# Attention loop: each head's sum, reciprocal, shares and transposes one step later, bias sums in odd steps

## The chip, the cores and the metric

The kernel runs on one core of one Trainium2 chip. The metric is the device time of one execution in microseconds (us). Engines are named as in the profile: PE (TensorE matmul), PEld (its weight loads), DVE (VectorE), ACT (ScalarE), POOL (GpSimd) and SP (SyncE, which issues the DMAs).

## The reference

Three stages stand one behind the other: attention with a position bias that a small network makes, a gated product with two weight matrices, and a block with softmax and layer norm. The attention has 2 batches, 8 heads, 576 positions and 64 dimensions per head; then there are 1152 rows of 512, with inner sizes 1536 and 1024.

```python
rel = pos[:, None] - pos[None, :]
x = (log1p(abs(rel)) / log1p(maximum(pos[:, None], 1)))[..., None]
bias = relu(x @ w1 + b1) @ w2                      # 1 -> 32 hidden -> 8 heads
scores = q @ k.T / sqrt(D) + bias.transpose(2, 0, 1)
attn = exp(scores - max); attn = attn / (attn.sum(-1) + 1e-9)
x = (attn @ v) as 1152 rows of 512
x = ((x @ w_a) * (x @ w_b)) @ w_out
h = x @ w_in;  solu = h * softmax(h)
out = (layer_norm(solu) * g_ln) @ w_out2
```

## The kernel before

**Tiles and heads.** The 576 query positions of a batch are four row tiles of 128 and a rest of 64. There are nine units: four row tiles times two batches, and one unit that holds the rests of both batches. A unit has eight heads, so the list `steps` holds 72 heads.

**The loop.** `for n in range(len(steps) + 5)` (L635) works on several heads at once. For each step n the string of letters in `ORDER` (L27) whose key is the largest that is at most n says which parts are issued and in which order. All engines take their instructions in the order in which they are issued, so the string sets the order on every engine. The letters:

- `s` scores of head n (L400, PE: tile `s`, two halves, with the high part `qhi` of q and its correction `qlo`);
- `b` biased, head n-1 (L419, DVE: adds `bias` to `s`, writes `e` and the row's extreme `nm`);
- `p` powers, head n-1 (L426, ACT: exponential in place, row sums);
- `a` summed_powers, head n-1 (L430, POOL: adds the small constant, tile `rec`);
- `h` shares, head n-2 (L435, DVE: reciprocal of `rec`; L436, POOL: multiplies `e`). In step 3, `g` and `f` make the sum and shares of an older head in an order of their own;
- `t` turned, head n-3 (PE transposes `pt` at L444 and, for the second head of a pair, `ptt` at L453; the copy `et` is ACT's for an even head, L447, DVE's for an odd one, L449; `ett` is ACT's, L455);
- `v` values, in odd steps: a pair of heads whose first is n-4 (L473, PE: tile `px`);
- `i` and `j`: high part (ACT, `xhi`, L479) and correction (DVE, `xlo`, L484) of a finished unit's output, in steps 4 mod 8;
- `k` and `l`: high part (`kst`, `qhi`) and correction (`qlo`, DVE, L327) of k and q for later units;
- `u` bias_sums and `o` bias_out: sums of a group of bias rows (L366, PE: tile `bps` from four tiles `h`), its store and its DMA;
- `x` everything else at that step's number: loads, copies of q and k (`nat_q` L280 on POOL, `nat_k` and `arena_hi` L277 and L278), their transposes `tp_q` and `tp_k` (L290), the bias network's hidden tiles `h` (L356 on DVE, L358 on ACT; two in step n-2 and two in n-1 for sums in step n), clearing of q tiles by POOL, and in the last unit the conversion of the first weights.

**What else sets the order.** A bias group's step is 16i + 2r, for the first row of groups a number from `SECOND_T`, for the last row one from `LAST_T` (L30, L31). The scores and the bias sums take turns in one PSUM pool of two buffers (`ps_s`); the later gated blocks `pm` use that pool too. Transposes have a pool of three buffers, `e` one of three, `et` one of two.

**End of the loop.** The weights come as 64-bit numbers, read as pairs of 32-bit words (`words`, L94) and rebuilt in single precision by ACT, POOL and DVE (L98, L102, L111, L113, L114); the first four pieces are rebuilt inside the loop by `first_one`, at the steps that `FIRST` lists (L609 and L611 make the high part and the correction, tile `first`). Three gated blocks `pm` (L132, 24 matmuls each, named by weight piece and row group) stand in the loop too, by `EARLY` in steps 72 (0,0), 74 (0,1) and 75 (1,0); their products are ACT's copy `one` (L151), DVE's `g` (L152), ACT's `gh` (L154) and DVE's `gl` (L156). Behind the loop the other weights are loaded into a pool that takes the attention's space, and blocks (1,1), (0,2), (1,2), (2,0) and so on follow.

Of the kernel before, what the change touches and what calls it, by code (L numbers as in the profile page):

```python
# [22 lines left out]

ORDER = {0: "kbvioljpatsxu", 2: "kbvioljptsxu", 3: "kbglfviojptshaxu", 4: "khbvioljpatsxu", 55: "khbilospajtvxu"}  # L27

KEYS = (4, 5, 6, 7, 7, 8, 9, 10, 11, 11)
SECOND_T = (5, 7, 9, 10, 12, 13, 14)  # L30
LAST_T = (48, 50, 52, 54)  # L31

HIDDEN = (("vvva", "vvva", "vvva", "vvva", "vvva", "vvva", "vvva", "vvva"),
          ("vvvv", "avvv", "avav", "avvv", "avav", "avvv", "avav", "avvv"), ("vvvv", "avvv"))
# [20 lines left out]
def tile_kernel(ctx, tc, q, k, v, w1, b1, w2, w_a, w_b, w_out, w_in2, w_out2, g_ln, psi, rpsi, out):  # L55
# [9 lines left out]
    NC = S // P  # L65
# [98 lines left out]
    with ExitStack() as actx:  # L164
# [56 lines left out]
        for g in range(4):  # L221
            r = slice(g * HID, (g + 1) * HID)
# [124 lines left out]
        def bias_hidden(T, quads=range(4)):  # L347

            it, r, c = place(T)
            for qd in quads:  # L350
                t0 = it * P + r + 16 * qd
                h = hp.tile([P, S], F32, tag="h", name=f"h_{T}_{qd}")
                win = tb[:, OFF - t0 - c:OFF - t0 - c + S]
                sc = nb[:, c, t0 // 16:t0 // 16 + 1]
                if HIDDEN[min(it, 2)][T % len(HIDDEN[min(it, 2)])][qd] == "v":
                    nc.vector.tensor_scalar(h, win, sc, 0.0, op0=ALU.add, op1=ALU.max)  # L356
                else:
                    nc.scalar.activation(h, win, AF.Relu, bias=sc)  # L358
                bias_w.setdefault(T, []).append(h)

        def bias_sums(T):

            bps = ps_s.tile([P, 2, 512], F32, tag="s", name=f"bps_{T}")
            for qd, h in enumerate(bias_w[T]):
                for a in range(2):
                    nc.tensor.matmul(bps[32 * qd:32 * qd + 32, a, 0:SH], w2bd, h[:, a * SH:(a + 1) * SH], start=True, stop=True)  # L366
            bias_w[T] = bps

        def bias_out(T, send=True):

            it, r, c = place(T)
            if it not in bias_t:
                bias_t[it] = big.tile([P, H, S], F32, tag="big", name=f"bias_{it}")
            st = stp.tile([P, S], F32, tag="st", name=f"st_{T}")
            k = 9 * c + 2 * it + r // 64
            nc.scalar.activation(st.rearrange("p (a j) -> p a j", a=2), bias_w.pop(T)[:, :, 0:SH], AF.Copy, scale=rp[:, k:k + 1])
            bias_w[T] = st
            if send:
                bias_sent(T)
# [78 lines left out]
        def values(u, p):  # L458

            it, bs = units[u]  # L460
            px = st_[u][0]
            et = [st_.pop(("et", u, 2 * p + j)) for j in range(2)]
            ett = st_.pop(("ett", u, p))
            n = P // len(bs)
            for c in range(NC + 1):
                for j, half in ((j, half) for j in range(2) for half in range(2)):

                    rows = slice(j * D + half * HID, j * D + (half + 1) * HID)
                    for m, b in enumerate(bs):
                        cols = slice(m * n, (m + 1) * n)  # L470
                        lhsT = (vsb[:, b, c] if c < NC else vtl[:, b])[:, p, j, half * HID:(half + 1) * HID]
                        rhs = et[j][:, c, cols] if c < NC else ett[:, cols]
                        nc.tensor.matmul(px[rows, p, cols], lhsT, rhs, start=(c == 0 and m == 0), stop=(c == NC), skip_group_check=True)  # L473
# [17 lines left out]
        def later(n, f, *args):  # L491
            extra.setdefault(n, []).append((f, args))
# [11 lines left out]
        for b in range(B):  # L504
            for g in range(2):
                i = b * 2 + g
# [72 lines left out]
            later(8 * (len(units) - 1) + j, clear_q, len(units) - 1, i // 4, i // 2 % 2, i % 2)  # L579
        for T in range(N0 + 1, S // 16):  # L580
            i, r = divmod(T - N0, N0)
            n = LAST_T[r] if i == NC - 1 else 16 * i + (SECOND_T[r - 1] if i == 0 else 2 * r)
            for g in range(2):
                if n - 2 + g < 0:
                    bias_hidden(T, (2 * g, 2 * g + 1))
                else:
                    later(n - 2 + g, bias_hidden, T, (2 * g, 2 * g + 1))
            sums_at.setdefault(n, []).append(T)
            out_at.setdefault(n + 1, []).append(T)
        steps = [(u, h) for u in range(len(units)) for h in range(H)]  # L590
# [29 lines left out]
        n = 8 * (len(units) - 1)  # L620
        later(LAST_T[-1] + 2, products_room)
        for i, stages in enumerate(FIRST):
# [8 lines left out]
        def at(f, n):  # L631
            if (0 <= n < len(steps)) and not (f is scores and n < 2):
                f(*steps[n])

        for n in range(len(steps) + 5):  # L635
            for part in ORDER[max(i for i in ORDER if i <= n)]:
                if part == "o":
                    for T in out_at.get(n, []):
                        bias_out(T)
                elif part in "ij":  # L640
                    if n >= 12 and n % 8 == 4:
                        (inputs_high if part == "i" else inputs_low)(n // 8 - 1)
                elif part in "kl":
                    for w in (keep_at if part == "k" else low_at).get(n, []):
                        (keep_high if part == "k" else keep_low)(w)
                elif part == "v":
                    if n >= 4 and n % 2 == 1:
                        u, h = steps[n - 4]
                        values(u, h // 2)
                elif part == "u":  # L650
                    for T in sums_at.get(n, []):
                        bias_sums(T)
                elif part == "x":
                    for f, args in extra.pop(n, []):
                        f(*args)
                else:
                    f, j = {"b": (biased, 1), "h": (shares, 2), "g": (shares, 3), "f": (summed_powers, 2), "p": (powers, 1), "a": (summed_powers, 1), "t": (turned, 3), "s": (scores, 0)}[part]
                    at(f, n - j)


# [46 lines left out]
    for s in range(NS):  # L707
        f = GS * (s + 1)
        if s == 0:
            pieces += [piece_ab(f, 0), piece_ab(f, 1)]  # L710
        n = ORDERED[s]
# [60 lines left out]
    for i in range(2):  # L772
        words, dst = stages[0].pop(0)
        f = stg.tile([P, NW], F32, tag="f", name="f")
# [44 lines left out]
    s = NS - 1  # L819
# [180 lines left out]
```

## Time and profile before

| | us |
|---|---|
| runs | 544.70, 543.47, 544.67 (median 544.67) |
| profiled execution, its own time | 544.01 |
| its span | 542.2 |

| engine | busy us | share of the span | instructions |
|---|---|---|---|
| PE | 530.4 | 98% | 4873 |
| PEld | 471.8 | 87% | 4873 |
| DVE | 419.1 | 77% | 904 |
| ACT | 286.1 | 53% | 598 |
| POOL | 156.5 | 29% | 262 |

The granted clock of PE is 1.00 over the whole span. Busy time is a sum over instructions; matmuls overlap and their ends are modelled, so a busy PE isn't PE at its peak. The attention loop ends at about 212; the rest of the span is the two blocks behind it. A row of the timeline gives the start, the duration of a run of equal instructions (x their number), the engine, the line, the operation, and output and inputs; in brackets the engine's idle time ahead of it and what released it.

### The profile page before, as it was taken

The numbers are of one execution on the slowest core, as the hardware profiler recorded it, in microseconds if no ns is written. First come the engines' busy times: TensorE is split into PE (matmuls) and PEld (weight loads), VectorE is DVE, ScalarE is ACT, GpSimd is POOL, SyncE is SP. The second block draws the span as 40 slices with busy tenths as digits, with TensorE's granted clock in tenths as the row PEclk, the third lists the DMA queues.
The fourth block names the chain that finished last, engine by engine and source line by source line (L and its number), as shares of the span: only waits on it lengthen the run. The fifth ranks groups of instructions, "written<-read, shape, count | busy, mean of one in ns | idle before, by whom it ended". The sixth has DMA issues, their size and how long they took to land.

```text
span 542.2 us, 12391 instructions
## 1 busy us (share of the span) xinstructions
PE 530.4 (98%) x4873; PEld 471.8 (87%) x4873; DVE 419.1 (77%) x904; ACT 286.1 (53%) x598; POOL 156.5 (29%) x262
## 2 busy tenths in 40 slices
PE   7989999999999999999999999999999999999997
PEld 3667788888878899999999999999999988888886
DVE  5988889999886794887899798897884467656661
ACT  5878887788886663555565334522534332232321
POOL 3034445554456630222222122242224330000000
PEclk9999999999999999999999999999999999999999
DMA  4995533333266012444553443444300000000011
GB/s 93 208 197 127 115 82 86 78 73 79 69 151 181 3 41 82 154 144 128 156 153 121 117 155 117 128 144 152 118 4 2 0 1 20 21 19 21 19 31 48
DMA packets 53918, 49.32 MB, mean 91 GB/s; under 512 B 31583, under 2 KB 44132, under 8 KB 53861
## 3 DMA queue, kind: packets, MB, share of 16 engines
q1 hardware_dynamic: 53584, 48.52, 33.1%
q8 instruction: 38, 0.62, 0.5%
q14 instruction: 20, 0.16, 0.1%
q10 hardware_dynamic: 276, 0.02, 0.0%
HBM read 34.37 MB, written 2.36 MB: 68 GB/s over the span
## 4 chain that ended last, share of the span: by engine, by line
PE 83%; DVE 8%; issue 3%; ACT 3%; POOL 1%; DMA 1%; SPq 0%; ACTq 0%; DVEq 0%; POOLq 0%
PE pm L132 26%; PE po L132 11%; PE py L897 9%; PE ph L837 9%; PE bps L366 6%; PE px L473 6%; PE s L400 5%; PE pt L444 5%; DVE e L419 2%; PE pl L878 1%; ACT e L426 1%; PE tp_q L290 1%; DVE et L449 1%; PE tp_k L290 1%; DMA arena_hi<-in_k_dram 1%
## 5 line engine op out<-in xcount | busy, mean ns | idle before, releaser
L102 POOL TENSOR_SCALAR f<-f 128x512 f32<-128x512 f32 x48 | 41.5, 866 | 138.3 <-ACT f L98 127.3
L132 PE MATMUL pm<-xhi,abh 128*128 128x384 f32 x240 | 80.2, 334 | 0.0
L132 PE MATMUL pm<-xhi,abl 128*128 128x384 f32 x240 | 80.2, 334 | 0.0
L132 PE MATMUL pm<-xlo,abh 128*128 128x384 f32 x240 | 80.2, 334 | 0.0
L426 ACT ACTIVATE e<-e,nm 128x576 f32<-128x576 f32 x72 | 56.0, 777 | 32.2 <-DVE nm L419 30.8
L436 POOL TENSOR_SCALAR e<-e,rec 128x576 f32<-128x576 f32 x72 | 53.8, 747 | 28.7 <-DVE rec L435 26.2
L419 DVE CUSTOM_DVE_ANT_0 e<-s,bias 128x576 f32<-128x576 f32 x72 | 53.9, 750 | 2.6 <-DMA arena_hi<-in_k_dram 1.3
L356 DVE TENSOR_SCALAR h<-tabs 128x576 f32<-128x576 f32 x116 | 55.0, 515 | 0.3
L132 PE MATMUL po<-gh,oh 128*128 128x384 f32 x144 | 48.5, 337 | 0.8 <-DVE x2s L768 0.8
L151 ACT COPY one<-pm 128x384 f32<-128x384 f32 x36 | 17.2, 478 | 60.9 <-PE pm L132 60.7
L132 PE MATMUL po<-gh,ol 128*128 128x384 f32 x144 | 48.4, 336 | 0.0
L132 PE MATMUL po<-gl,oh 128*128 128x384 f32 x144 | 48.4, 336 | 0.0
L366 PE MATMUL bps<-h,w2bd 128*32 128x288 f32 x576 | 45.7, 420 | 1.2 <-DVE h L356 1.0
L444 PE MATMUL pt<-ident,e 128*128 128x128 f32 x288 | 45.1, 279 | 0.4 <-POOL e L436 0.4
L132 PEld LDWEIGHTS pm<-xhi,abl 128*128 128x128 f32 x240 | 45.1, 188 | 0.0
L132 PEld LDWEIGHTS pm<-xhi,abh 128*128 128x128 f32 x240 | 45.0, 188 | 0.0
L132 PEld LDWEIGHTS pm<-xlo,abh 128*128 128x128 f32 x240 | 45.0, 188 | 0.0
L114 DVE SCALAR_TENSOR_TENSOR f<-words,f 128x512 int32<-128x512 int32 x48 | 42.8, 891 | 1.6
L430 POOL TENSOR_SCALAR rec<-sums 128x1 f32<-128x1 f32 x72 | 20.9, 290 | 79.2 <-ACT e L426 78.9
L400 PE MATMUL s<-kst,qhi 128*128 128x288 f32 x160 | 40.6, 335 | 2.4 <-DVE nm L419 2.4
L473 PE MATMUL px<-et,vsb 128*32 128x128 f32 (+1 forms) x1280 | 40.5, 264 | 0.2 <-DVE et L449 0.2
L473 PEld LDWEIGHTS px<-et,vsb 128*32 128x32 f32 x1280 | 33.8, 110 | 7.5 <-issue 2.1
(137 smaller groups left out, 1247.8 us busy)
## 6 DMA issues: line engine op xcount, KB each, us to landing
bias<-st SPq DMA_DIRECT2D x40, 288.0 KB, 3.6
words<-in_moe_w_out_dram SPq DMA_DIRECT2D x20, 512.0 KB, 3.6
words<-in_moe_w_a_dram SPq DMA_DIRECT2D x12, 512.0 KB, 3.6
words<-in_moe_w_b_dram SPq DMA_DIRECT2D x12, 512.0 KB, 3.4
words<-in_moe_w_in_dram SPq DMA_DIRECT2D x8, 512.0 KB, 3.7
nat_q<-in_q_dram SPq DMA_DIRECT2D x16, 128.0 KB, 3.2
arena_hi<-in_k_dram SPq DMA_DIRECT2D x16, 128.0 KB, 2.5
vsb<-in_v_dram SPq DMA_DIRECT2D x16, 128.0 KB, 2.6
```

What stands on the lines that cost most here:

```text
L114: nc.vector.scalar_tensor_tensor(out=b, in0=words[:, :, 0], scalar=29, in1=b, op0=ALU.logical_shift_right, op1=ALU.bitwise_or)
L132: nc.tensor.matmul(ps, w, x, start=(i == 0), stop=(i == n - 1))
L356: nc.vector.tensor_scalar(h, win, sc, 0.0, op0=ALU.add, op1=ALU.max)
L366: nc.tensor.matmul(bps[32 * qd:32 * qd + 32, a, 0:SH], w2bd, h[:, a * SH:(a + 1) * SH], start=True, stop=True)
L400: nc.tensor.matmul(ps[:, a, 0:SH], w, kst[:, b, h, a * SH:(a + 1) * SH], start=(m == 0), stop=(m == len(mm) - 1))
L419: nc.vector.tensor_tensor_reduce(out=halves(e), in0=ps[:, :, 0:SH], in1=halves(bias_t[it][:, h, :]), op0=ALU.add, op1=ALU.min, scale=1.0, ...
L426: nc.scalar.activation(e, e, AF.Exp, bias=nm, scale=-1.0, accum_out=sums[:, h:h + 1])
L436: nc.gpsimd.tensor_scalar(e, e, rec[:, h:h + 1], 1.0, op0=ALU.mult, op1=ALU.mult)
L444: nc.tensor.transpose(pt[:, c, :], e[:, j * TL + c * P:j * TL + (c + 1) * P], ident)
L473: nc.tensor.matmul(px[rows, p, cols], lhsT, rhs, start=(c == 0 and m == 0), stop=(c == NC), skip_group_check=True)
L837: nc.tensor.matmul(ph[u][:, a], x[:, kc, cols], w[:, kc, a * 512:(a + 1) * 512], start=(i == 0), stop=(i == 3 * KD - 1))
L897: nc.tensor.matmul(ps, x[:, c, :], w[:, c, cols], start=(i == 0), stop=(i == 3 * KF - 1))
```

## The change

The sum of a head's powers is issued two steps behind its scores in place of one, the reciprocal and the shares three in place of two, the transposes four in place of three, the values in even steps, for the pair whose first head is n-5, and a unit's high part and correction in steps 5 mod 8. The loop has one step more. The letters `g` and `f` are gone, and the strings have a new order: shares `h` and sum `a` stand at the head of a step (from step 4 on), `k` right behind them. Bias sums stand at 16i + 2r - 1, those of the last row one step earlier; `SECOND_T`, `FIRST`, `EARLY`, `HIDDEN` and the steps of the loads and of the transposes of q and k keep their numbers. The changed file has one line less ahead of the loop, so its line numbers are lower by one.

```diff
-ORDER = {0: "kbvioljpatsxu", 2: "kbvioljptsxu", 3: "kbglfviojptshaxu", 4: "khbvioljpatsxu", 55: "khbilospajtvxu"}
+ORDER = {0: "hakbvioljptsxu", 3: "kbhavioljptsxu", 4: "hakbvioljptsxu", 55: "hakbilospjtvxu"}
-LAST_T = (48, 50, 52, 54)
+LAST_T = (47, 49, 51, 53)
-            n = LAST_T[r] if i == NC - 1 else 16 * i + (SECOND_T[r - 1] if i == 0 else 2 * r)
+            n = LAST_T[r] if i == NC - 1 else 16 * i + (SECOND_T[r - 1] if i == 0 else 2 * r - 1)
-        for n in range(len(steps) + 5):
+        for n in range(len(steps) + 6):
-                    if n >= 12 and n % 8 == 4:
+                    if n >= 13 and n % 8 == 5:
-                    if n >= 4 and n % 2 == 1:
-                        u, h = steps[n - 4]
+                    if n >= 6 and n % 2 == 0 and n - 5 < len(steps):
+                        u, h = steps[n - 5]
-                    f, j = {"b": (biased, 1), "h": (shares, 2), "g": (shares, 3), "f": (summed_powers, 2), "p": (powers, 1), "a": (summed_powers, 1), "t": (turned, 3), "s": (scores, 0)}[part]
+                    f, j = {"b": (biased, 1), "h": (shares, 3), "p": (powers, 1), "a": (summed_powers, 2), "t": (turned, 4), "s": (scores, 0)}[part]
```

In the rows of order below a tile's name ends with a number of its own; the numbers ahead of it are the unit and the head (`pt_0_3` is unit 0, head 3), for `nat_q` and `tp_q` the unit, the group of heads and the batch.

**First place:** PE in step 6, where the first q piece of unit 1 is transposed; before:

```order
L444 MATMUL pt_0_3_664<-ident_72,e_0_2_524 128x128 x4
L453 MATMUL ptt_0_1_671<-ident_72,e_0_2_524 128x128
L400 MATMUL s_0_6_675<-kst_161,qhi_0_1_0_521 128x288 x2
L400 MATMUL s_0_6_675<-kst_161,qlo_0_1_0_522 128x288 x2
L290 MATMUL tp_k_1_0_2_680<-ident_72,arena_hi_164 128x128 x4
L290 MATMUL tp_q_1_0_0_691<-ident_72,nat_q_1_0_0_492 128x128 x4
L473 MATMUL px_0_427<-et_0_2_624,vsb_162 32x128 x2
```

And after the change:

```order
L443 MATMUL pt_0_2_654<-ident_72,e_0_2_524 128x128 x4
L399 MATMUL s_0_6_661<-kst_161,qhi_0_1_0_521 128x288 x2
L399 MATMUL s_0_6_661<-kst_161,qlo_0_1_0_522 128x288 x2
L289 MATMUL tp_k_1_0_2_666<-ident_72,arena_hi_164 128x128 x4
L289 MATMUL tp_q_1_0_0_677<-ident_72,nat_q_1_0_0_491 128x128 x4
L443 MATMUL pt_0_3_698<-ident_72,e_0_2_524 128x128 x4
L452 MATMUL ptt_0_1_705<-ident_72,e_0_2_524 128x128
```

The transposes of head 3 stood ahead of `tp_q` and now stand behind it; those of head 2 have come into this step. On POOL, around the copy `nat_q` that these transposes read, before:

```order
L436 TENSOR_SCALAR e_0_2_524<-e_0_2_524,rec_0_429 128x576
L430 TENSOR_SCALAR rec_0_429<-sums_0_428 128x1
L436 TENSOR_SCALAR e_0_2_524<-e_0_2_524,rec_0_429 128x576
L430 TENSOR_SCALAR rec_0_429<-sums_0_428 128x1
L280 TENSOR_SCALAR nat_q_1_0_0_492<-nat_q_1_0_0_492 128x4x64
L436 TENSOR_SCALAR e_0_4_594<-e_0_4_594,rec_0_429 128x576
```

And after the change:

```order
L435 TENSOR_SCALAR e_0_2_524<-e_0_2_524,rec_0_429 128x576
L429 TENSOR_SCALAR rec_0_429<-sums_0_428 128x1
L279 TENSOR_SCALAR nat_q_1_0_0_491<-nat_q_1_0_0_491 128x4x64
L435 TENSOR_SCALAR e_0_2_524<-e_0_2_524,rec_0_429 128x576
L429 TENSOR_SCALAR rec_0_429<-sums_0_428 128x1
L435 TENSOR_SCALAR e_0_4_581<-e_0_4_581,rec_0_429 128x576
```

The copy has moved ahead of the share of head 3 (the second row of `e_0_2`).

**Second place:** DVE in unit 3, a step of 5 mod 8 with the start of the next, where `xlo` stands; before, from the step ahead of it:

```order
L419 ISA e_3_2_1691,nm_3_3_1738<-s_3_3_1727,bias_1_424 128x576
L419 ISA nm_3_3_1738 128x1
L484 TENSOR_TENSOR xlo_1016<-px_2_1222,xhi_1015 128x4x128
L449 COPY et_3_1_1749<-pt_3_1_1744 128x512
L356 TENSOR_SCALAR h_23_1_1762<-tabs_104 128x576
L435 RECIPROCAL rec_3_1578<-rec_3_1578 128x1
L419 ISA e_3_4_1775,nm_3_4_1776<-s_3_4_1755,bias_1_424 128x576
L419 ISA nm_3_4_1776 128x1
L356 TENSOR_SCALAR h_23_2_1818<-tabs_104 128x576
L356 TENSOR_SCALAR h_23_3_1820<-tabs_104 128x576
L435 RECIPROCAL rec_3_1578<-rec_3_1578 128x1
L419 ISA e_3_4_1775,nm_3_5_1824<-s_3_5_1810,bias_1_424 128x576
```

And after the change:

```order
L418 ISA e_3_4_1767,nm_3_4_1768<-s_3_4_1755,bias_1_424 128x576
L418 ISA nm_3_4_1768 128x1
L483 TENSOR_TENSOR xlo_1043<-px_2_1225,xhi_1042 128x4x128
L448 COPY et_3_1_1778<-pt_3_1_1773 128x512
L355 TENSOR_SCALAR h_24_0_1792<-tabs_104 128x576
L355 TENSOR_SCALAR h_24_1_1794<-tabs_104 128x576
L434 RECIPROCAL rec_3_1580<-rec_3_1580 128x1
L418 ISA e_3_4_1767,nm_3_5_1808<-s_3_5_1784,bias_1_424 128x576
L418 ISA nm_3_5_1808 128x1
```

`xlo`, the copy `et` of an odd head and the first two hidden tiles of a bias group (`h_24_0`, `h_24_1`) now stand between two `biased` instructions in one step; before, `xlo` and that `et` stood with one hidden tile between two `biased` instructions, and `h_24_0` and `h_24_1` came two steps later.

**Third place:** DVE at the end of the loop, behind the conversions of step 72; before, from the last of the six rows of conversions (ahead of the first of them stood the copy `et_8_5`):

```order
L114 SCALAR_TENSOR_TENSOR single_3_3625<-words_3_3460,single_3_3625 128x512
L435 RECIPROCAL rec_8_3267<-rec_8_3267 128x1
L152 TENSOR_TENSOR g_0_0_3727<-pm_0_0_3652,one_0_0_3726 128x384
L156 TENSOR_TENSOR gl_0_3651<-g_0_0_3727,gh_0_3650 128x384
L449 COPY et_8_7_3737<-pt_8_7_3732 128x512
L611 TENSOR_TENSOR first_3553<-single_2_3556,first_3553 128x512
L611 TENSOR_TENSOR first_3553<-single_3_3625,first_3553 128x512
```

And after the change:

```order
L113 SCALAR_TENSOR_TENSOR single_3_3575<-words_3_3444,single_3_3575 128x512
L434 RECIPROCAL rec_8_3238<-rec_8_3238 128x1
L448 COPY et_8_5_3671<-pt_8_5_3666 128x512
L151 TENSOR_TENSOR g_0_0_3678<-pm_0_0_3638,one_0_0_3677 128x384
L155 TENSOR_TENSOR gl_0_3637<-g_0_0_3678,gh_0_3636 128x384
L434 RECIPROCAL rec_8_3238<-rec_8_3238 128x1
L448 COPY et_8_7_3763<-pt_8_7_3758 128x512
L610 TENSOR_TENSOR first_3539<-single_2_3542,first_3539 128x512
L610 TENSOR_TENSOR first_3539<-single_3_3575,first_3539 128x512
```

The reciprocal behind the conversions was that of head 71 and is now that of head 70; the copy `et` of head 69 (`et_8_5`) has moved behind the conversions, and head 71's reciprocal behind the first product. On PE, the transposes of head 71 and what follows them after the change:

```order
L131 MATMUL pm_0_1_3733<-xlo_1043,first_3539 128x384
L131 MATMUL pm_0_1_3733<-xhi_1042,first_3539 128x384
L443 MATMUL pt_8_7_3758<-ident_72,e_8_6_3547 128x128 x4
L452 MATMUL ptt_8_3_3765<-ident_72,e_8_6_3547 128x128
L131 MATMUL pm_1_0_3780<-xhi_1042,first_3539 128x384
L131 MATMUL pm_1_0_3780<-xlo_1043,first_3539 128x384
L131 MATMUL pm_1_0_3780<-xhi_1042,first_3539 128x384 x2
L131 MATMUL pm_1_0_3780<-xlo_1043,first_3539 128x384
```

Before, the block `pm_0_1` and the last values stood between these transposes and `pm_1_0`; now `pm_1_0` follows at once, and the last values stand behind it.

## Rows read from the trace of the kernel before

**Rows 1.** Busy time by stretch: stretch, length, PE, PEld, DVE, ACT, POOL, clock, DMA.

```profile
62.35:157.33 94.98, 94.80 (x1519) 78.83 (x1517) 86.66 (x228) 76.43 (x168) 47.12 (x91) 1.00 0.37 88
157.33:212.37 55.04, 53.92 (x890) 47.99 (x888) 39.95 (x102) 34.23 (x83) 24.99 (x53) 1.00 0.26 69
```

**Rows 2.** Timeline of PE, a pair of steps in the stretch with bias sums.

```profile
98.65 1.20 PE L366 MATMUL bps<-h,w2bd 128*32 128x288 f32 x16
99.65 1.13 PE L473 MATMUL px<-et,vsb 128*32 128x128 f32 x32
...
100.93 0.66 PE L444 MATMUL pt<-ident,e 128*128 128x128 f32 x4
...
101.95 0.60 PE L444 MATMUL pt<-ident,e 128*128 128x128 f32 x4
...
103.56 1.20 PE L366 MATMUL bps<-h,w2bd 128*32 128x288 f32 x16
```

**Rows 3.** Timeline of DVE, one step of the same stretch.

```profile
97.69 0.76 DVE L419 CUSTOM_DVE_ANT_0 e<-s,bias 128x576 f32<-128x576 f32 x1
...
98.37 0.69 DVE L484 TENSOR_TENSOR xlo<-px,xhi 128x512 fp32r<-128x512 f32 x1
98.97 0.68 DVE L449 COPY et<-pt 128x512 f32<-128x512 f32 x1
...
103.49 0.94 DVE L356 TENSOR_SCALAR h<-tabs 128x576 f32<-128x576 f32 x2
```

**Rows 4.** Waits of the whole run: engine and line, releaser, us, count, longest.

```profile
DVE rec L435 <- POOL rec L430: 15.6, 29, 1.3
```

**Rows 5.** Timeline of PE behind the bias sums: first of four pairs, and their end.

```profile
161.52 0.53 PE L400 MATMUL s<-kst,qhi 128*128 128x288 f32 x2 [0.36 <-DVE nm L419]
...
162.68 1.08 PE L473 MATMUL px<-et,vsb 128*32 128x128 f32 x32
...
166.14 1.08 PE L473 MATMUL px<-et,vsb 128*32 128x128 f32 x32
...
178.53 1.08 PE L473 MATMUL px<-et,vsb 128*32 128x128 f32 x32
```

**Rows 6.** Timeline of all engines at the first q transposes of unit 1.

```profile
40.77 0.42 POOL L280 TENSOR_SCALAR nat_q<-nat_q 128x256 f32<-128x256 f32 x1 [2.32 <-DMA nat_q<-in_q_dram]
...
41.17 0.76 POOL L436 TENSOR_SCALAR e<-e,rec 128x576 f32<-128x576 f32 x1
...
41.24 0.66 PE L290 MATMUL tp_q<-ident,nat_q 128*128 128x128 f32 x4 [0.63 <-POOL nat_q L280]
```

**Rows 7.** Timeline of all engines at the end of the attention loop.

```profile
198.07 1.41 DVE L611 TENSOR_TENSOR first<-single,first 128x512 fp32r<-128x512 f32 x2
...
204.49 0.69 DVE L114 SCALAR_TENSOR_TENSOR single<-words,single 128x512 int32<-128x512 int32 x1
...
205.10 0.15 DVE L435 RECIPROCAL rec<-rec 128x1 f32<-128x1 f32 x1
...
206.15 0.66 PE L444 MATMUL pt<-ident,e 128*128 128x128 f32 x4 [0.27 <-POOL e L436]
...
206.68 0.42 PE L132 MATMUL pm<-xhi,first 128*128 128x384 f32 x1
...
211.04 1.12 PE L473 MATMUL px<-et,vsb 128*32 128x64 f32 x62
```

**Rows 8.** Chain that ended last: start, us, instructions of gated blocks behind the last values.

```profile
212.44 29.33 PE pm L132 x168
```

**Rows 9.** Timeline of all engines, the weights behind the loop.

```profile
212.48 0.37 SPq L94 DMA_DIRECT2D words<-in_moe_w_a_dram  x1
...
220.24 0.68 ACT L98 ACTIVATE f<-words 128x512 f32<-128x512 f32 x1 [0.59 <-DMA words<-in_moe_w_out_dram]
...
221.05 0.48 ACT L151 COPY one<-pm 128x384 f32<-128x384 f32 x1
...
222.35 0.54 DVE L152 TENSOR_TENSOR g<-pm,one 128x384 f32<-128x384 f32 x1
```

## Prediction

> **What bounds the kernel now.** I read the stretches first, since the change touches only the attention loop. In the stretch with bias sums (62.35 to 157.33) PE is busy 94.80 of 94.98 us, DVE 86.66; in the stretch after them PE has 53.92 of 55.04 and DVE falls to 39.95 [rows 1]. A busy PE need not be at its peak, so I then read PE's own sequence in one pair of steps [rows 2]: sums at 98.65, values at 99.65, transposes at 100.93, scores and the next transposes by 101.95, scores and a q transpose, and the next sums at 103.56. The reader is to see starts that follow each other with no releaser and no idle time worth naming: 1.00 + 1.28 + 1.02 + 1.61 = 4.91 us of pure work. There PE is the bound, and a longer pipeline can't shorten it; it can only disturb it.
>
> DVE is close behind. One step's list [rows 3]: `biased` 0.68 (97.69 to 98.37), `xlo` 0.60 (to 98.97), `et` 0.68, two `h` 0.94. That DVE waits 15.6 us in 29 places for POOL's `rec` [rows 4] is what the change attacks: the reciprocal of head n-2 stands at the head of DVE's step and waits for a sum that POOL made one engine hop earlier. In the bias stretch those waits lie beside PE's work. In the stretch behind it they don't: `s` starts at 161.52 after an idle 0.36 put down to DVE, and four pairs from 162.68 to 178.53 take 15.85 us, where the first of them (162.68 to 166.14) takes 3.46 [rows 5].
>
> **The change, term by term.** No instruction is added or removed; PE's list has the same matmuls. So the sum is over waits that go and waits that come, against the profiled execution's own 544.01 us (span 542.2); the median of the runs shown is 0.66 higher, inside the range.
>
> *Waits that go.* Two of the four pairs hold a q transpose, about 0.4 each (part of the 1.61 of [rows 2]), so 15.85 - 4 x 3.46 - 0.8 = 1.2 of waits, and the 0.36: 1.6 us. With `rec` made two steps before its reciprocal DVE does not stand at it any more. What is late next there is nothing on PE's side for some steps, but POOL still makes its share (0.76 [rows 6]) and a sum in each step of some 2 us and has memsets besides, so I leave 0.4: **-1.2 us** (bounds -1.6 and -0.8).
>
> *Fill.* In step 6 PE transposes unit 1's first q piece. It stood idle until 41.24 because POOL's copy came at 40.77, when the load landed [rows 6]; the load's place in SP's queue does not move. So PE is pinned there in both kernels, and all that stands behind it counts in full. Before, the transposes of head 3 were ahead of that point; now they are behind it: 0.5. POOL's copy now stands ahead of head 3's share, which therefore ends at 41.17 + 0.76 = 41.93, while PE is free about 41.77: 0.2 more. **+0.7 us** (0 if the load lands earlier; 1.2 if DVE's work of these steps, one `et` later, also slips). ACT's load of steps 8 to 12 stays the same but for one copy; I take the waits up to 62 as unchanged.
>
> *Bias stretch.* Before, the odd head's `et` copy and the q correction `qlo` lay in steps of different parity. Now both lie in odd steps, and so do `xlo` and the first two `h` of an even bias group (second place in the section on the change): in steps of 5 mod 8 DVE must do 0.68 + 0.60 + 0.60 + 0.94 and then the next `biased`, 0.68 and some 0.1 for its reciprocal: 3.6 us [rows 3], and it can start only about 0.2 after the previous scores. PE wants the buffer that this second `biased` frees after the odd step's transposes, scores and sums (1.1 + 1.0), values (1.28) and the even step's transposes (0.4): 3.8 [rows 2]. With 0.2 for the signal DVE is there at 4.0. Six such steps at 0.2: 1.2. In the 12 steps with `qlo` the copy `et` ends about 2.1 into the step, when values want it: 0 to 0.1 each, 0.3 taken for all. Together **+1.5 us**. Bounds: 0, since the steps of even parity are light (1.7 us of DVE) and may lend time; 4.5, if each of the six loses 0.45 and each of the 12 loses 0.15. I stay nearer the lower end because a 0.60 `xlo` ahead of `et` stood in one step in eight before as well, and values still started at 99.65, when `et` (98.97 + 0.68) ended [rows 3].
>
> *Drain, reciprocal behind conversions.* In step 72 DVE converts the first weights; its last conversion begins at 204.49, the reciprocal follows at 205.10 and, behind POOL's share, PE's transposes of head 71 at 206.15, after 0.27 idle [rows 7]. Now the reciprocal behind that block is head 70's. Behind that PE had transposes 0.5 (206.15 to 206.68), a gated block, values 1.4 (211.04 [rows 7] to 212.44 [rows 8]) and a gated block; a block is 24 matmuls, 4.2 us (168 in 29.33 [rows 8]): 10.3 us. Now it has both heads' transposes, two values and both blocks: 12.2. DVE reaches the conversions' end one `et` (0.6) sooner. **+1.3 us** (0.6 if PE's earlier gain carries over to DVE, 1.9 if that `et` brings nothing).
>
> *Drain, a gated block behind a copy.* Block pm_1_0 stood behind the last values; now it stands right behind the transposes of head 71 (third place). Its third matmul needs the low part `first`, which on DVE stands behind `et` of head 71. From the end of the transposes: 0.2 signal, 0.6 `et`, 0.7 for one `first` (half of 1.41 [rows 7]), 0.2 signal, less two matmuls (0.35): **+1.3 us** (0.6 to 1.6).
>
> *Weights behind the last values.* The first `words` DMA is issued at 212.48, right as the last values end, and ACT waited for the third of them until 220.24 [rows 9]: 7.8 us after the values. Only then ACT copies `one` and DVE multiplies at 222.35, which frees the buffer of pm_1_1. Before, pm_1_0 ran first behind the values, then pm_1_1 and pm_0_2, so that pm_1_2, which takes that buffer, was due 3 x 4.2 = 12.6 us after them; now it is due after 8.4. By the durations of these rows [rows 9] the product can't end before 7.8 + 0.68 + 0.48 + 0.54 = 9.5, plus 0.3 for two signals, 9.8: **+1.4 us** (0.4 to 1.8; the lower end if the transfers land sooner).
>
> Sum: -1.2 + 0.7 + 1.5 + 1.3 + 1.3 + 1.4 = +5.0, so 549.0 us. All low ends give 544.0 (-1.6 + 0 + 0 + 0.6 + 0.6 + 0.4 = 0), all high ends 554.2 (-0.8 + 1.2 + 4.5 + 1.9 + 1.6 + 1.8 = 10.2).
>
> *Is PE really full there?* PE's starts follow each other without a gap in the bias stretch [rows 2], and I count no headroom. The Trainium skill (Perfetto Trace Analysis, Identifying the Most-Contended Engine) speaks against that reading: matmul busy time is no measure of how near PE is to its roofline, and the busy share of weight loads is to be used instead. By that rule the stretch has headroom, and the change could be worth far more than my sum grants; it is the fourth rival, and I give it little, since the pair of 4.91 us adds up from its parts.
>
> **Rivals.**
> 1. *Faster: the reciprocal loop paces more than I grant.* If two thirds of the 15.6 us of DVE's waits [rows 4] lay on the path, 10.4 would go in place of 1.2, and 544.0 - 10.4 + 6.2 = 539.8 would come out. For it: DVE is 91% busy in the bias stretch, and each wait delays `biased`. Against it: PE's unbroken starts there, and an excess of only 1.6 in the stretch where PE does wait. It wins from the point where the gain passes the 6.2 of new waits. Chance 0.08.
> 2. *No change.* The bias stretch absorbs its new order (0), the gated block finds its low part early (0.6), and the transfers land sooner (0.4): -1.2 + 0.7 + 0 + 1.3 + 0.6 + 0.4 = +1.8, and less with the fill at its low end: 544.0 to 545.8. For it: light even steps on DVE. Chance 0.20.
> 3. *Much slower: DVE becomes the bound.* If the 18 heavy odd steps each lose 0.45, that is 8.1 in place of 1.5: 555.6. For it: 91% busy. Against it: DVE's total is unchanged and a light step follows at once. Chance 0.09.
> 4. *Faster: PE's matmuls in the bias stretch are packed in appearance only.* Weight loads are busy 78.83 of 94.98 us there [rows 1]. Were the rest, 16.1 us, waiting that the longer pipeline frees, 549.0 - 16.1 = 532.9 would come out. Chance 0.03.
>
> That the change doesn't do what it says: the sums of the first row of bias groups keep their step numbers, three of seven in even steps. That is a matter of a few 0.1 us, inside the terms.
>
> **How the numbers follow.** My case has 0.60; the likeliest time is 549.0. I leave out rivals 1 and 4 below (0.11) and rival 3 above (0.09), which is 0.20, and keep the whole of my case with its bounds and of no change: 544.0 to 554.2. A difference of 0.3% (1.6 us) is what a measurement of this kernel can tell from none. Faster by more has 0.08 + 0.03 = 0.11, within it 0.20, slower 0.60 + 0.09 = 0.69.
>
> **What would show it.** In the changed profile: DVE's waits for POOL's `rec` gone, pairs of 3.5 to 3.9 us behind the bias stretch; PE still idle at unit 1's first q transpose; short PE waits for DVE once in eight steps; transposes of head 70 waiting for POOL; pm_1_0 starting with two matmuls and a stop of about 1 us; the third block behind the last values waiting for DVE's product. I am wrong if the bias stretch gets shorter than 95 us for the same steps, or if the last three waits don't appear.

## The result, and the profile after

The kernel after takes 548.01 us (median of 6 runs, 547.40 to 548.70), the kernel before 544.10 (6 runs, 542.92 to 545.05): a ratio of 1.0074, 95% interval 1.0057 to 1.0091. It is slower by 3.9 us; 549.0 was predicted, with a range of 544.0 to 554.2. The profiled execution after took 547.66 us, its span is 545.9, and the granted clock is 1.00 as before.

PE's busy time is the same (530.6 us against 530.4), so the loss is waiting. To find its place I compare when PE starts the scores of the same head in both traces, and take out the work that now stands ahead of or behind that point: a bias sum is 0.99 us, the transposes of one head about 0.5. The last row is `po`, the first matmul behind the gated blocks of the first weights. (The values of step n are those of the pair whose second head is n-4 before and n-5 after; the sections on the kernel and on the change call it the first.)

| start of | before | after | difference | work ahead only after | lost so far | lost in the part |
|---|---|---|---|---|---|---|
| scores of head 0 | 24.39 | 25.06 | 0.67 | 0 | 0.67 | |
| scores of head 16 | 69.97 | 72.54 | 2.57 | 0.99 - 0.47 | 2.05 | 1.4 (fill) |
| scores of head 54 | 158.82 | 160.68 | 1.86 | 0.99 - 0.47 | 1.34 | -0.7 (bias sums) |
| scores of head 71 | 196.17 | 196.15 | -0.02 | -0.5 | 0.5 | -0.8 (behind them) |
| first `po` | 241.60 | 245.47 | 3.87 | 0 | 3.9 | 3.4 (drain) |

The 0.67 at the start isn't the change's: in two kernels below that differ from the kernel after only in the drain, that point lies at 24.29 (prod_first) and 25.42 (all_three). Without it the parts sum to 3.3 us; the interval of the ratio is 3.1 to 5.0.

**Most of the waits that were attacked are gone.** From the waits of the whole run after (engine and line, releaser, us, count, longest), to be held against [rows 4]:

```profile
POOL e L435 <- DVE rec L434: 82.0, 64, 3.9
...
DVE rec L434 <- POOL rec L429: 3.4, 7, 0.5
```

DVE waits 3.4 us in 7 places for POOL's sum, in place of 15.6 in 29. POOL now waits for DVE instead (82.0 us in 64 places, 26.2 in 46 before). Most of that costs PE nothing; in two places, the shares of head 1 and of head 70, PE waits in turn for POOL (0.68 and 0.73, below).

**Bias sums.** PE, then DVE, in the timeline after, where `xlo`, the odd head's `et` and two `h` stand in one step (the second place of the change):

```profile
101.03 0.60 PE L443 MATMUL pt<-ident,e 128*128 128x128 f32 x4
...
102.20 1.20 PE L365 MATMUL bps<-h,w2bd 128*32 128x288 f32 x16
103.19 1.13 PE L472 MATMUL px<-et,vsb 128*32 128x128 f32 x32
...
104.47 0.66 PE L443 MATMUL pt<-ident,e 128*128 128x128 f32 x4
104.88 0.51 PE L399 MATMUL s<-kst,qhi 128*128 128x288 f32 x2
```

```profile
101.23 0.76 DVE L418 CUSTOM_DVE_ANT_0 e<-s,bias 128x576 f32<-128x576 f32 x1 [0.35 <-PE s L399]
...
101.91 0.69 DVE L483 TENSOR_TENSOR xlo<-px,xhi 128x512 fp32r<-128x512 f32 x1
102.52 0.68 DVE L448 COPY et<-pt 128x512 f32<-128x512 f32 x1
103.11 0.94 DVE L355 TENSOR_SCALAR h<-tabs 128x576 f32<-128x576 f32 x2
...
104.71 0.08 DVE L418 DVE_READ_ACCUMULATOR2_ANT nm<- 128x1 f32 x1
```

DVE starts this list 0.20 after the previous scores (101.03) and frees the buffer at 104.79; PE wants it at 104.88 and doesn't wait.

**Fill.** PE after:

```profile
35.03 0.66 PE L443 MATMUL pt<-ident,e 128*128 128x128 f32 x4 [0.68 <-POOL e L435]
36.22 0.33 PE L452 MATMUL ptt<-ident,e 128*128 128x128 f32 x1 [0.54 <-ACT et L446]
...
41.12 0.60 PE L289 MATMUL tp_q<-ident,nat_q 128*128 128x128 f32 x4
...
63.09 0.50 PE L399 MATMUL s<-kst,qhi 128*128 128x288 f32 x2 [0.76 <-DVE nm L418]
```

The q transposes at 41.12 don't wait, unlike [rows 6]: POOL's copy began at 39.81, 3.9 us after its load was issued (5.5 before). PE waits elsewhere: for the share of head 1, for ACT's copy `et`, and at step 13 for DVE.

**Drain.** PE after; [rows 7] and [rows 8] answer to it:

```profile
199.97 0.46 PE L472 MATMUL px<-ett,vtl 128*32 128x64 f32 x16 [0.20 <-ACT ett L454]
...
206.07 0.66 PE L443 MATMUL pt<-ident,e 128*128 128x128 f32 x4 [0.73 <-POOL e L435]
...
212.98 0.34 PE L131 MATMUL pm<-xlo,first 128*128 128x384 f32 x1
214.24 0.61 PE L131 MATMUL pm<-xhi,first 128*128 128x384 f32 x2 [0.92 <-DVE first L610]
...
218.26 1.11 PE L472 MATMUL px<-et,vsb 128*32 128x64 f32 x62
...
228.72 0.44 PE L131 MATMUL pm<-xhi,first 128*128 128x384 f32 x1 [0.54 <-DVE g L151]
```

Three stops stand where they were predicted: head 70's transposes wait for POOL, `pm_1_0` stops behind its second matmul, and the third block behind the last values waits for DVE's product.

The last of the three isn't the same in every execution. Five profiled kernels have this drain (after, even_sums, second11, second3, fill_share); from the scores of head 71 to the first `po` they take 49.23 to 49.63 us, and fill_share 50.42, where the third block waits 1.60 in place of 0.40 to 0.79 and ACT gets the third transfer 8.4 us after the first was issued (7.2 to 7.6 in the others). The drain of the kernel before takes 45.43 or 45.44 in before, before_odd and middle, though the third transfer came as late as 8.1 in middle: there one block more stood behind the last values. So a difference below 1 us in the drain of a single trace shows little.

### The profile page after: what moved, and what is told of

Same layout as the page of the kernel before. It is cut to its first block, busy times and chain, and to the rows that moved or that the text cites. A ratio compares the mean times of both kernels' runs of the same rounds, so it can differ in the third digit from the quotient of the medians.

```text
span 545.9 us, 12383 instructions
## 1 busy us (share of the span) xinstructions
PE 530.6 (97%) x4873; PEld 471.8 (86%) x4873; DVE 415.9 (76%) x904; ACT 288.6 (53%) x598; POOL 152.5 (28%) x262
## 4 chain that ended last, share of the span: by engine, by line
PE 87%; DVE 5%; ACT 4%; issue 2%; DMA 2%; SPq 1%; POOL 0%; DVEq 0%; ACTq 0%
PE pm L131 25%; PE po L131 11%; PE py L896 9%; PE ph L836 9%; PE bps L365 8%; PE px L472 7%; PE s L399 6%; PE pt L443 5%; PE tp_q L289 1%; PE pl L877 1%; PE tp_k L289 1%; DMA words<-in_moe_w_out_dram 1%; ACT e L425 1%; PE table L209 1%; DVE e L418 1%
## 5 line engine op out<-in xcount | busy, mean ns | idle before, releaser
L97 ACT ACTIVATE f<-words 128x512 f32<-128x512 f32 x48 | 32.5, 677 | 19.0 <-DMA words<-in_moe_w_a_dram 8.9
L443 PEld LDWEIGHTS pt<-ident,e 128*128 128x128 f32 x288 | 32.9, 140 | 8.3 <-issue 4.5
```

What stands on the lines that cost most here:

```text
L443: nc.tensor.transpose(pt[:, c, :], e[:, j * TL + c * P:j * TL + (c + 1) * P], ident)
```

## The experiments

Each kernel was timed in five rounds beside the kernel before, so the last column is what counts; after stands at +3.9.

| label | edit | median us | before, same chip | difference | ratio, interval |
|---|---|---|---|---|---|
| late_conv | drain | 548.01 | 543.79 | +4.2 | 1.0079 (1.0065 to 1.0092) |
| low_early | drain | 546.55 | 543.79 | +2.8 | 1.0055 (1.0042 to 1.0069) |
| prod_first | drain | 550.79 | 543.79 | +7.0 | 1.0126 (1.0110 to 1.0142) |
| all_three | drain | 550.19 | 543.79 | +6.4 | 1.0122 (1.0107 to 1.0136) |
| prod_head | drain | 548.11 | 544.09 | +4.0 | 1.0072 (1.0059 to 1.0085) |
| drain_best | drain | 545.99 | 543.68 | +2.3 | 1.0046 (1.0031 to 1.0060) |
| even_sums | sums | 560.26 | 544.09 | +16.2 | 1.0296 (1.0282 to 1.0311) |
| before_odd | sums | 552.52 | 544.09 | +8.4 | 1.0155 (1.0141 to 1.0168) |
| fill_share | fill | 548.41 | 544.09 | +4.3 | 1.0074 (1.0060 to 1.0089) |
| second11 | fill | 549.22 | 543.68 | +5.5 | 1.0097 (1.0080 to 1.0114) |
| second3 | fill | 550.42 | 543.68 | +6.7 | 1.0114 (1.0098 to 1.0131) |
| middle | both ends | 544.21 | 543.98 | +0.2 | 1.0004 (0.9995 to 1.0013) |

**The low part earlier.** On the kernel after:

```diff
-... (1, 6, 7, 8, 10, 11), (4, 7, 8, 8, 11, 11))
+... (1, 6, 7, 8, 10, 10), (4, 7, 8, 8, 10, 10))
```

> The changed kernel with the low part of the first weights made in step 74 in place of 75, so that on DVE it stands ahead of the copy et of head 71. Theory: block pm_1_0 no longer stops behind its second matmul, 1.1 us go: 546.9 us (546.6 to 547.3). Rival (the loss lies ahead of the drain): 548.0.

1.1 us of the loss went by the medians (+3.9 to +2.8), and the stop at `pm_1_0` with it (PE):

```profile
205.78 0.66 PE L443 MATMUL pt<-ident,e 128*128 128x128 f32 x4 [0.73 <-POOL e L435]
...
227.56 0.44 PE L131 MATMUL pm<-xhi,first 128*128 128x384 f32 x1 [0.85 <-DVE g L151]
```

The other two stops are left, the last one longer (0.85 for 0.54), so that from head 71 to the first `po` the trace gains 0.8. The stop at `pm_1_0` has an idle 0.92 in each of the five kernels with the drain of the kernel after and is absent here: that `first` behind `et` cost about 1 us is shown.

**The conversions a step later.**

```diff
-... (1, 6, 7, 8, 10, 11), (4, 7, 8, 8, 11, 11))
+... (1, 6, 7, 9, 10, 11), (4, 7, 9, 9, 11, 11))
```

> The changed kernel with the last weight conversions of step 72 put into step 73, so that the reciprocal of head 70 stands ahead of them. Theory (the lost time lies in the drain): the transposes of head 70 no longer wait 0.73 us for POOL, and the wait of 0.2 for ett behind it goes: 547.0 us (546.6 to 547.4). Rival (the loss lies ahead of the drain, in the fill or in the stretch with bias sums, and the drain only waits for what comes late anyway): 548.0, no change.

Nothing was gained. Head 70's transposes (204.93) don't wait any more, but PE stands still later, at head 71's:

```profile
204.93 0.60 PE L443 MATMUL pt<-ident,e 128*128 128x128 f32 x4
...
211.87 0.66 PE L443 MATMUL pt<-ident,e 128*128 128x128 f32 x4 [0.41 <-POOL e L435]
...
213.91 0.62 PE L131 MATMUL pm<-xhi,first 128*128 128x384 f32 x2 [0.93 <-DVE first L610]
...
229.56 0.44 PE L131 MATMUL pm<-xhi,first 128*128 128x384 f32 x1 [1.70 <-DVE g L151]
```

From the scores of head 71 to that second stop it is 18.01 us here and 18.09 after. The stops of the drain aren't independent: DVE's list of conversions, copies and low parts sets when `first` is there, and a stop ahead of it is only part of that time. (The 1.70 at the third block is mostly the transfer's: ACT waited 2.06 for it.)

**The product of block (1,1) sooner.** First ahead of the third transfer only, alone and with the two edits above; then ahead of all three, with the low part earlier:

```diff
 prod_first, all_three (in the loop over blocks)
+            own = s == 0 and w == (1, 1)
...
-            for g in (pr, cv, cv, pr, cv, pr):
+            for g in (pr, pr, pr, cv, cv, cv) if own else (pr, cv, cv, pr, cv, pr):
...
 prod_head
+    gated(1, 1)
+    products(1, 1)
     for i in range(2):
...
         words, dst = stages[0].pop(0)
```

> The changed kernel with the product of block (1,1) issued right behind the block, ahead of the conversion that waits for the third weight transfer. Theory: block pm_1_2 no longer waits for DVE's product, 0.7 us go: 547.3 us (547.0 to 547.6). Rival: the product now delays the conversions of the next weights, and block (2,0) waits in its place: 548.0 to 549.

> The three edits of the drain together: reciprocal ahead of the conversions, low part ahead of et, product of block (1,1) at once. Theory (all of the loss is in the drain, the longer pipeline itself costs and gains nothing): 548.0 - 1.0 - 1.1 - 0.7 = 545.2, or, if the drain holds the whole difference, 544.1, as before the change. Rival (the loss lies ahead of the drain): 547 or more.

> The changed kernel with the low part of the first weights made in step 74 (as in the run with that edit alone, 546.55 us) and the block (1,1) with its product issued ahead of all conversions of the later weights. Theory (block pm_1_2 waits 0.85 us because ACT's copy of block (1,1) stands behind transfers): 545.7 (545.4 to 546.1). Rival (the conversions come later and block pm_2_0 waits for them or for the product of (0,2), as in the run that moved the product behind two of them): 547 or more.

All three theories missed, the first two by far; the last two times lie in the range of their rivals. In the run with the three edits ACT's copy `one` still stood behind the second transfer, and that came 8.0 us after the last values (218.83 to 226.81), later than the third in the kernel after (7.4):

```profile
222.93 0.66 ACT L97 ACTIVATE f<-words 128x512 f32<-128x512 f32 x1 [3.23 <-DMA words<-in_moe_w_a_dram]
226.81 0.66 ACT L97 ACTIVATE f<-words 128x512 f32<-128x512 f32 x1 [3.21 <-DMA words<-in_moe_w_b_dram]
227.37 0.46 ACT L150 COPY one<-pm 128x384 f32<-128x384 f32 x1
```

DVE, in turn, held its conversions back behind that product, and block (2,0) then waited 2.68 us at 235.62. With the product ahead of all transfers the wait of `pm_1_2` did go, and the next block waited:

```profile
232.23 0.44 PE L131 MATMUL pm<-xhi,abh 128*128 128x384 f32 x1 [1.27 <-DVE g L151]
```

That is the rival: once the weights land, DVE has conversions and products to make, and PE has one block less behind the last values to wait with.

**A drain laid out anew.** Conversions in step 71, low part and the product of `pm_0_0` in 74, `pm_0_1` in 75 and `pm_1_0` in 76:

```diff
-... (1, 6, 7, 8, 10, 11), (4, 7, 8, 8, 11, 11))
+... (1, 6, 7, 7, 10, 10), (4, 6, 7, 7, 10, 10))
-EARLY = {(0, 0): 8, (0, 1): 10, (1, 0): 11}
+EARLY = {(0, 0): 8, (0, 1): 11, (1, 0): 12}
-            later(n + m + 1, products, c, tg)
+            later(n + (10 if tg == 0 and c == 0 else m + 1), products, c, tg)
```

> The changed kernel with its drain laid out anew: the last weight conversions in step 71, so that only the reciprocal of head 69 stands behind them; the low part of the first weights in step 74; block (0,1) behind the transposes of head 71, block (1,0) behind the last values as before the change; the product of (0,0) in step 74. Theory (three stops in the drain hold the loss): no wait of the transposes of head 70 for POOL (1.0 us), none for the low part (1.4, as the run with that edit alone gave), none of block pm_1_2 for a product (0.8): 548.0 - 3.2 = 544.8 (544.0 to 545.6). Rival (DVE's work between the last scores and the weights behind the loop sets the end, so that a stop taken away comes back as another): 546.5 or more.

546.0, between the theory and its rival: 1.6 us of the 3.9 went. Seven blocks again stand behind the last values, and from the first of them to the first `po` it is 29.23 us as before (214.38 to 243.61; 212.37 to 241.60). But the conversions now hold up `biased` of head 71 (203.89 in place of 200.59 after), and with it ACT and POOL:

```profile
200.16 0.46 PE L472 MATMUL px<-ett,vtl 128*32 128x64 f32 x16 [0.80 <-ACT ett L454]
...
206.25 0.66 PE L443 MATMUL pt<-ident,e 128*128 128x128 f32 x4 [0.62 <-POOL e L435]
```

**Bias sums in even or odd steps.** On the kernel after, and the reverse on the kernel before:

```diff
-LAST_T = (47, 49, 51, 53)
+LAST_T = (48, 50, 52, 54)
-... 2 * r - 1)
+... 2 * r)
```

> The changed kernel with the bias sums back in even steps (step numbers and those of the last row as before the change). The prediction's term (odd steps too heavy for DVE cost 1.5 us): 546.5. Theory formed from the trace after (PE waits nowhere in that stretch, so DVE has room): 548.0 (547.6 to 548.4). Rival (sums in the step in which the values stand hurt): slower, 548.5 to 550.

> The kernel before with the bias sums in odd steps and nothing else of the change. If the 0.7 us that PE gained between steps 16 and 54 come from the odd sums: 543.4. If they come from the longer pipeline: 544.1 or slower, since the sums now stand in the steps of the values, up to 546.

Both became much slower, 12.3 and 8.4 us, and no theory had that size. The loss lies among the bias sums: from the scores of head 16 to those of head 54 it is 100.49 us with even sums (88.14 after) and 97.06 with odd sums in the kernel before (88.85). PE in the changed kernel with even sums:

```profile
100.00 0.51 PE L399 MATMUL s<-kst,qhi 128*128 128x288 f32 x2
...
100.71 1.17 PE L472 MATMUL px<-et,vsb 128*32 128x128 f32 x30
...
102.14 0.66 PE L443 MATMUL pt<-ident,e 128*128 128x128 f32 x4
...
103.25 1.20 PE L365 MATMUL bps<-h,w2bd 128*32 128x288 f32 x16
104.38 0.65 PE L443 MATMUL pt<-ident,e 128*128 128x128 f32 x4
104.88 0.27 PE L452 MATMUL ptt<-ident,e 128*128 128x128 f32 x1
104.90 0.51 PE L399 MATMUL s<-kst,qhi 128*128 128x288 f32 x2
...
106.36 0.96 PE L472 MATMUL px<-et,vsb 128*32 128x128 f32 x26 [0.18 <-DVE et L448]
```

A pair of steps without q transposes takes 4.90 us here (100.00 to 104.90) and up to 5.44; in the kernel after such a pair takes 4.41 to 4.47. PE shows no idle time for most of it. There the values follow the sums at once, since the sums end an odd step and the values begin the next, and sums take 0.99 and values 1.28 at most (102.20, 103.19 and 104.47 above). Here transposes and scores lie between: sums take 1.13 (103.25 to 104.38) and values 1.43 or more (100.71 to 102.14), and both scores of the pair, not one, are followed by matmuls of 32 columns, which makes them 0.1 longer. Part of the 1.43 is a wait: without the sums ahead of them the values come while DVE's `et` is still being copied (106.36). How the 12.3 us divide between the two wasn't measured alone. An estimate from the pair shown: about 0.15 of its 0.45 is the wait (1.43 for 1.28), so some 0.3 in each of 19 pairs, about 6 us, would be the neighbours, and the rest waits, for `et` above all, which the time of the sums covers in the kernel after.

So the odd sums are no part of the loss. With them the values can move to even steps.

**The fill.** Share of head 1 in step 3; then the bias group of step 12 in 11; then the first groups in odd steps:

```diff
 fill_share
-... 3: "kbhavioljptsxu", 4: "hakbvioljptsxu", 55 ...
+... 3: "kbhaviolgjptsxu", 4: "akbvioljptsxu", 5: "hakbvioljptsxu", 55 ...
-... "h": (shares, 3), ...
+... "h": (shares, 3), "g": (shares, 2), ...
 second11, second3
-SECOND_T = (5, 7, 9, 10, 12, 13, 14)
+SECOND_T = (5, 7, 9, 10, 11, 13, 14)
+SECOND_T = (3, 5, 7, 9, 11, 13, 14)
```

> The changed kernel with the share of head 1 made in step 3, one step sooner, and every other head as it was. Theory (in the fill the longer pipeline costs PE a wait of 0.68 us for that share): 547.3 (547.0 to 547.7). Rival (the wait only moves to the next one, of ptt for ACT's copy et, 0.54): 548.0.

> The changed kernel with the bias group of step 12 in step 11. Theory (in the fill the sums of step 12 stand apart from values, and the next scores wait 0.76 us for a biased instruction that stands behind a hidden tile): the wait goes and the sums stand beside values: 547.0 (546.6 to 547.4). Rival (steps 9 to 11 then hold three groups in a row and the wait comes there): 548.0 or more.

> The changed kernel with the first row of bias groups in steps 3, 5, 7, 9, 11, 13 and 14, six of seven odd. Theory (in the fill, too, sums stand best in the step ahead of values): 546.5 (546.0 to 547.2). Rival (DVE and ACT have no room for four hidden tiles in steps 1 and 2, where keys and queries are brought in): 548.5 or more.

All three went to the rivals. With the earlier share the wait of 0.68 went, and the next grew from 0.54 to 1.36:

```profile
36.56 0.33 PE L452 MATMUL ptt<-ident,e 128*128 128x128 f32 x1 [1.36 <-ACT et L446]
```

With the sums moved to step 11, PE waits at 63.93 for `xlo` and `et` (0.48 and 0.18) in place of 0.76 at step 13; with a group in step 3 keys and queries are brought in later, and one `tp_k` waits 2.16 for `qlo`. The profiled execution with the group in step 11 has the span of the kernel after (545.9), while its median lies 1.6 us further from the kernel before; why its other runs were longer stays open.

**The longer pipeline in the middle only.** The kernel before, with the change's order, offsets and odd sums in steps 14 to 56 alone:

```diff
+... 14: "kbvioljpsxu", 15: "HAkbvioljpTsxu", 55: "HAkbilospjTvxu",
+56: "AHhkbilospajTtvxu", 57: "khbilospajtvxu"}
...
+                    late = 14 <= n < 57
+                    if n >= 4 and n % 2 == (0 if late else 1) and n != 14:
+                        u, h = steps[n - (5 if late else 4)]
+... "H": (shares, 3), "A": (summed_powers, 2), "T": (turned, 4) ...
```

> The longer pipeline and the odd sums only in steps 14 to 56, with the fill (steps 0 to 13) and the drain (from step 57) of the kernel before. Theory (by the traces the change costs 1.4 us in the fill and 3.4 us in the drain and gains 0.7 us between steps 16 and 54): 544.1 - 0.7 = 543.4 (542.8 to 544.2). Rival (the longer pipeline itself costs time in the stretch of the loop that it stays in, or each of the two turns between the forms costs a step's wait): 545.5 to 547.

544.21 against 543.98: no difference that can be measured, so the loss is gone, and the gain that was expected didn't come. Between the scores of heads 16 and 54 it keeps what the kernel after had won (88.12 us; 88.85 before, 88.14 after), and from head 71 to the first `po` it takes 45.44, as before (45.43). The gain is given back where the forms meet. From head 0 to head 16 it takes 47.56, as long as the kernel after (47.48; 45.58 before, all with the same work but for the 0.5 of the table): entering the longer pipeline in step 14, with a fill like the old one, cost as much as entering it in the fill. In step 14, three sums in a row (PE):

```profile
65.97 0.53 PE L401 MATMUL s<-kst,qhi 128*128 128x288 f32 x2 [0.97 <-ACT st L377]
```

and in step 56, where two heads are turned at once, 0.54 for POOL's share. No version beat the kernel before. The new order of the letters within a step wasn't tried without the longer pipeline.

## Why the prediction was right

The sign, the time and the place of most of the loss came out; two terms of six were wrong, and the time is near in part by luck, since their errors cancel.

- **Waits that go** (-1.2, bounds -1.6 and -0.8): -0.8 behind the bias sums and -0.7 among them, 1.5 in all. That the stretch with sums would give nothing, since PE's starts followed each other there [rows 2], was wrong by 0.7, and with it came one of the prediction's own signs of being wrong: for the same work the stretch got shorter. [rows 2] shows one pair of 19. Four others (from heads 20, 36, 48 and 52) took 0.13 to 0.27 longer than the same pairs after. In the first of them the values start at 80.92, before the odd head's copy `et` ends on DVE (81.07), and it is 1.42 to the next transposes in place of 1.28; after the change `et` ends as they start (84.60, 84.59).
- **Fill** (+0.7, bounds 0 and 1.2): 1.4, above its bounds and for other reasons. The step that failed is that PE is pinned to the load of the q piece. The load came 1.6 us sooner after its issue and pinned nothing, the case for which the term had 0. PE waits at the share of head 1, at the copies behind it and at step 13; the three edits of the fill moved these waits and removed none of the loss. That any entry into the longer pipeline costs this much is what the run in the middle suggests, with one trace.
- **Bias stretch** (+1.5, bounds 0 and 4.5): nothing was lost. DVE's list took 3.56 us as worked out (101.23 to 104.79), but PE took the buffer 0.09 after its end, where 0.2 had been added for a signal, and wanted it 3.85 after the previous scores: a tie, not a wait of 0.2. Worse, I weighed the odd sums as a burden on DVE and did not see that they keep sums and values side by side on PE, and give `et` the time of the sums; the two runs put both together at 8 to 12 us.
- **Reciprocal behind conversions** (+1.3): from the scores of head 71 to the start of `pm_1_0` PE has one head's transposes more, 0.53, than before up to the last values; 16.57 - 0.53 - 14.87 = 1.2 us of stops. But late_conv took the cause away and this time stayed (18.01 for 18.09 to the second stop): the size came out, the cause isn't the reciprocal alone.
- **Gated block behind a copy** (+1.3): 1.1 (212.98 + 0.18 to 214.24), and 1.1 by the medians of the run that took it away.
- **Weights behind the last values** (+1.4, bounds 0.4 and 1.8): 0.7. The third transfer came 7.4 us after the values (7.8 in [rows 9]) and ACT was quicker behind it, so the block started 9.1 us after them and not 9.8. In the five executions with this drain the block's wait goes up to 1.60, within the bounds.

As the terms stand it was 5.0 forecast; these readings sum to 2.9, the parts of the table to 3.3, the medians to 3.9. Most of what the readings leave out is at `pm_1_0`, which now stands between transposes and values and takes 5.54 us (212.72 to 218.26) where a block among blocks takes 4.18 and the stop 1.08. The missing 1.5 of the bias stretch and the smaller last term were made up in part by the fill.

Of the rivals, no change had the bias stretch right (0), but took the fill and the drain too low. DVE did not become the bound. The Trainium skill's rule (Perfetto Trace Analysis, Identifying the Most-Contended Engine) to judge TensorE's headroom by MFU (the share of peak arithmetic that the kernel does) and the busy share of its weight loads had left, by the second measure, 16.1 us of headroom among the bias sums; this case's trace doesn't bear that out for a longer pipeline, which won 0.7 us there.

My first theory behind the result, that the drain holds separate stops which can be taken away one by one, fell: only the low part's did. That is also what the prediction's sum did when it added three drain terms. What the runs fit is one list of DVE work between the last scores and the new weights, of which PE meets now one end and now the other; no run made that list shorter, so this is argued and not shown.

## What to carry to other kernels

A longer software pipeline pays in its steady part, here 1.5 us in steps 16 to 71, and is paid for at both ends, here 1.4 and 3.4 us, so cost the fill and the drain before the middle. Read every pair of steps before calling an engine full, not one. Ahead of moving an operation by a step, look at what stands beside it on the bound engine and not only at the engine that it loads. In a drain, find the engine whose list links the stops before counting them one by one.

## What the runs showed of the hardware

Matmuls that fill 32 columns (`bps`, `px`) cost more next to those of 128 columns than next to each other: sums took 0.99 us with values behind them and 1.13 with transposes, and scores took 0.61 ahead of transposes and 0.70 ahead of sums. So in these rows a change of form costs about 0.1 us on either side, with no idle time in the trace. The Trainium skill (TensorEngine Tiling (Array Packing), Key Properties) says that changing the tiling mode drains the TensorE; the rows agree in direction and give it a price; no run shows the drain itself.

The same load of a q piece took 3.9 us in one kernel and 5.5 in the other, and in all_three, of four weight loads issued together, ACT got the second 7.5 us after its issue (219.29 to 226.81).
